# Feed-forward sums turned by VectorE in 32x32 blocks, stored in 128-byte pieces, with units of 960 tokens in a row

## The chip, the core and the metric

The kernel runs on one core of one Trainium2 chip. The metric is the time of one execution in microseconds (us), the median of three runs. The core has TensorE (PE in the profile, with PEld for its weight loads), VectorE (DVE), ScalarE (ACT), GpSimd (POOL) and SyncE (SP), which here issues all DMA transfers. SBUF is the working memory, PSUM the memory that TensorE writes.

## The reference

The input x has 4 batches of 12480 tokens with 128 features; there are 32 inducing vectors. All is in float32.

```python
def mab(q, kv):
    s = scale * (q @ kv.transpose(0, 2, 1))
    s = s - s.max(-1, keepdims=True)
    a = np.exp(s)
    a /= a.sum(-1, keepdims=True) + 1e-09
    return a @ kv
h = mab(I, x)                      # first attention: 32 inducing vectors over 12480 tokens
y = mab(x, h).reshape(49920, 128)  # second attention: each token over the 32 rows of h
hid = np.maximum(y @ w_in, 0.0)    # feed-forward, 128 -> 2048
out = (hid * hid) @ w_out          # 2048 -> 128
```

## The kernel before

The 49920 tokens are cut into 52 units of 960, 13 per batch. A unit is two blocks of 480 tokens. For each unit there are three stages.

First attention (class `First`): x is loaded as a tile xn of 120 partitions with 8 tokens each, turned by TensorE to xt (features on partitions; L463, copied by L270), scored against the inducing vectors (L478), exponentiated with a running maximum, turned back (L512) and multiplied with xn (L536). After the 13th unit of a batch `first_end` joins the parts to hT, and folds it into the feed-forward's first weights: hw = hT x w_in (L632 to L641). Second attention (class `Second`) scores a unit's tokens against hT (L674), evicts and turns the scores (ss, L693), does the softmax with 120 tokens on the partitions (L700 to L721, tile d, whose last product is L721), and turns it back (PE ap, L752). A high part of the result in reduced-precision float (fp32r) and the low remainder go to sw (L270 and L762). Sixteen small DMAs (L768) copy sw, over partitions, into st: four times the 32 weights of a token, high and low, stacked on 128 partitions. Feed-forward (`ffn_block`): for each block, 16 matmuls h (L896) of 480 columns read st and hw; ScalarE applies relu (L908) and the square (L924) to g; VectorE splits g into hi (L929) and lo (L934); 48 matmuls (L973) sum hi x wo_hi, hi x wo_lo and lo x wo_hi into one PSUM bank op, features on partitions.

What then happens to op is what the change touches. `done` copies op to SBUF (ot, by ScalarE or VectorE, L270), `turn` turns it on TensorE with four transposes (otp, L993), `turned` copies them to osb on VectorE (L270), and once both blocks of a unit are there, `store` writes the unit with one DMA (L1007). In the last unit the blocks are stored apart (L1011), and the very last block is handled in two halves (L1021 to L1039).

Tokens are numbered so that a partition of xn and osb holds 8 tokens that follow one another in memory:

```python
x_v = x.rearrange("b (p j) c -> b p j c", p=TS)             # L228, TS = 120
out_v = out.rearrange("(b p j) c -> b p j c", b=B, p=TS)    # L229
```

so a load and a store move 120 pieces of 4 KB per unit. The two blocks of a unit take alternate groups of 120 tokens, which is why an h matmul reads st in four runs (`s["st", u][:, :, k, :]`).

The order of the work on every engine is written out ahead by a planner (class `Plan`, `run` at L84). Each piece of work is added with its engine or a choice of engines ("ACT|DVE"), an assumed length in ns, what it needs, which buffers it takes, and a due time. The planner picks for each engine, among what can start, the piece with the earliest due time. Due times of unit w hang on `t_main + w * PERIOD`, with PERIOD 32000. The numbers are only for ordering: on the chip each engine runs its list in order and waits on semaphores. SP too runs its list in order, so a DMA that waits holds those behind it. The program gives its DMAs eight semaphores in turn, and a DMA waits until the one eight places ahead of it has landed.

Second attention of a unit is started only once the first h matmul of the unit before it has been issued (`begun`, in `narrow`); its st is needed by that next unit's first h matmul. st and the output tiles have two buffers each, as has op.

## Time and profile before

| | |
|---|---|
| median of 3 runs | 1729.77 us (1728.26 to 1730.32) |
| profiled execution, its span | 1730.0 us |
| granted TensorE clock, mean | 0.995 |
| PE busy | 1706.0 us, 99% of the span |
| DVE busy | 1651.4 us, 95% |
| ACT busy | 1605.6 us, 93% |
| DMA packets | 56935, 82.06 MB, 18.1% of 16 engines on SP's queue |

A row of the groups gives line, engine, operation, tiles as written <- read, shape, count, then the busy time in us, the mean ns of one, and the idle time ahead of them. The chain of waits is followed back from the last instruction; its rows give start, length and what held the time. A window row gives for a stretch the busy time of each engine (and the number of instructions), the granted clock, the DMA engines' share and GB/s. A timeline row gives start and length in us. SPq is the issue of a DMA by SP.

### The profile page before, as it was taken

The page shows a single profiled execution, that of the slowest core. Times are in us where ns is not written, and L with a number is a line of the kernel's source. Part 1 is how long each engine was busy: PE and PEld are TensorE (multiplying, and loading weights), DVE is VectorE, ACT ScalarE, POOL GpSimd, SP SyncE. Part 2 cuts the span into 40 slices and gives each one's busy share as a digit, 9 for nine tenths or more (in the row PEclk, how much of TensorE's full clock was granted, in tenths as well). Part 3 has the DMA queues.
Part 4 walks back from the last instruction along what each step waited for, and adds up shares of the span by engine and source line. Part 5 has one row for each costly group of instructions (what it writes and reads, how often), then busy time and mean ns, then how long its engine had stood idle before and what let it go on. Part 6 is the DMA issues. An engine that isn't in the chain of part 4 may idle for free.

```text
span 1730.0 us, 25326 instructions
## 1 busy us (share of the span) xinstructions
PE 1706.0 (99%) x9527; PEld 1416.2 (82%) x9527; DVE 1651.4 (95%) x1734; ACT 1605.6 (93%) x1686; POOL 58.3 (3%) x57
## 2 busy tenths in 40 slices
PE   7899999999999999999999999999999999999998
PEld 5588888888788888888878888888887888888887
DVE  5999999999999999999999999999999999999998
ACT  6699999999989999999988999999998999999997
POOL 0000000000000000000000000000000000000000
PEclk9899999999999999999999999999999999999999
DMA  9121111111121111111212111111110111111010
GB/s 234 51 55 47 51 43 44 52 45 43 36 57 47 50 43 46 52 45 43 53 29 58 49 43 47 51 44 44 42 28 24 35 35 40 30 37 33 24 46 23
DMA packets 56935, 82.06 MB, mean 47 GB/s; under 512 B 14790, under 2 KB 43942, under 8 KB 56814
## 3 DMA queue, kind: packets, MB, share of 16 engines
q1 hardware_dynamic: 56814, 80.46, 18.1%
q8 instruction: 75, 1.23, 0.3%
q14 instruction: 46, 0.38, 0.1%
HBM read 29.77 MB, written 25.56 MB: 32 GB/s over the span
## 4 chain that ended last, share of the span: by engine, by line
PE 94%; DVE 2%; ACT 1%; DMA 1%; SPq 1%; issue 0%; ACTq 0%; DVEq 0%
PE op L973 61%; PE h L896 21%; PE otp L993 3%; PE xtp L463 2%; PE na L674 2%; PE nb L536 1%; PE na L478 1%; PE ep L512 1%; PE s2t L693 1%; PE ap L752 1%; PE wp L632 1%; DVE lo L934 0%; SPq L768 0%; DVE hi L929 0%; PE sp L478 0%
## 5 line engine op out<-in xcount | busy, mean ns | idle before, releaser
L934 DVE TENSOR_TENSOR lo<-g,hi 128x1920 fp32r<-128x1920 f32 (+1 forms) x419 | 895.2, 2137 | 16.8 <-DVE hi L929 0.5
L908 ACT ACTIVATE g<-h 128x960 f32<-128x960 f32 x832 | 794.7, 983 | 62.5 <-PE h L896 60.8
L924 ACT ACTIVATE g<-g 128x1920 f32<-128x1920 f32 (+1 forms) x419 | 758.8, 1811 | 4.0
L896 PE MATMUL h<-st,hw 128*128 128x480 f32 x1664 | 523.5, 392 | 2.4 <-DMA st<-sw 1.2
L929 DVE CAST hi<-g 128x1920 fp32r<-128x1920 f32 (+1 forms) x419 | 480.0, 1146 | 20.0 <-PE op L973 9.6
L973 PE MATMUL op<-hi,wo_lo 128*128 128x480 f32 x1664 | 495.7, 383 | 0.0
L973 PE MATMUL op<-hi,wo_hi 128*128 128x480 f32 x1664 | 458.8, 386 | 0.0
L973 PE MATMUL op<-lo,wo_hi 128*128 128x480 f32 x1664 | 436.6, 382 | 0.0
L973 PEld LDWEIGHTS op<-lo,wo_hi 128*128 128x128 f32 x1664 | 311.4, 188 | 52.6 <-issue 1.0
L973 PEld LDWEIGHTS op<-hi,wo_lo 128*128 128x128 f32 x1664 | 308.9, 188 | 53.0 <-issue 4.6
L896 PEld LDWEIGHTS h<-st,hw 128*128 128x128 f32 x1664 | 303.0, 189 | 57.1 <-issue 11.7
L973 PEld LDWEIGHTS op<-hi,wo_hi 128*128 128x128 f32 x1664 | 304.1, 188 | 45.9 <-issue 0.9
L715 POOL TENSOR_SCALAR z<-z 120x8 f32<-120x8 f32 x51 | 57.6, 1130 | 1606.6 <-DVE z L711 1606.6
L270 DVE COPY osb<-otp 120x512 f32<-120x512 f32 x103 | 70.2, 682 | 0.1
L463 PE MATMUL xtp<-ident,xn 120*128 120x120 f32 x416 | 61.9, 276 | 4.3 <-DMA xn<-in_x_dram 3.6
L463 PEld LDWEIGHTS xtp<-ident,xn 120*128 120x128 f32 x416 | 51.2, 146 | 17.5 <-issue 3.7
L993 PE MATMUL otp<-ident,ot 128*120 128x128 f32 x412 | 61.8, 272 | 0.5 <-DVE ot L270 0.5
L993 PEld LDWEIGHTS otp<-ident,ot 128*120 128x120 f32 x412 | 50.4, 137 | 12.8 <-DVE ot L270 1.5
L270 ACT COPY xt<-xtp 128x480 f32<-128x480 f32 x71 | 40.3, 572 | 13.4 <-PE xtp L463 13.4
L270 ACT COPY ot<-op 128x480 f32<-128x480 f32 x65 | 37.1, 570 | 0.8 <-PE op L973 0.8
L536 PE MATMUL nb<-xn,et 120*32 120x128 f32 x752 | 34.1, 280 | 0.0
L674 PE MATMUL na<-xt,hT 128*32 128x240 f32 x416 | 32.7, 387 | 0.4 <-DVE hT L270 0.4
(117 smaller groups left out, 650.6 us busy)
## 6 DMA issues: line engine op xcount, KB each, us to landing
xn<-in_x_dram SPq DMA_DIRECT2D x52, 480.0 KB, 4.3
st<-sw SPq DMA_DIRECT2D x816, 30.0 KB, 1.9
out_dram<-osb SPq DMA_DIRECT2D x51, 480.0 KB, 3.4
hi_i<-in_moe_w_in_dram SPq DMA_DIRECT2D x2, 512.0 KB, 13.5
lo_i<-in_moe_w_in_dram SPq DMA_DIRECT2D x2, 512.0 KB, 15.6
hi_o<-in_moe_w_out_dram SPq DMA_DIRECT2D x2, 512.0 KB, 11.9
lo_o<-in_moe_w_out_dram SPq DMA_DIRECT2D x2, 512.0 KB, 9.8
out_dram<-osb SPq DMA_DIRECT2D x1, 240.0 KB, 2.6
```

Of the source, the lines that this page charges most:

```text
L270: ENG[task.by](dst, src)
L463: nc.tensor.transpose(v["tp"][:, t * TS:(t + 1) * TS], self.xn[:, 4 * k + t, :], ident[:TS, :TS])
L536: nc.tensor.matmul(where[q * M:(q + 1) * M, :], self.et[:, k, q * M:(q + 1) * M], self.xn[:, 2 * q + k, :], start=(k == 0), stop=(k == 1),)
L674: nc.tensor.matmul(where[q * M:(q + 1) * M, :], self.s["hT"][:, :M], self.s["xt"][self.u][:, q * 2 * TS:(q + 1) * 2 * TS], start=True, sto ...
L715: E.tensor_scalar(v["z"], v["z"], 1e-9, 0.0, ALU.add, ALU.add)
L896: nc.tensor.matmul(c["hp"][:, l, :BLK].rearrange("p (q t) -> p q t", q=Q), s["hw"][:, f * P:(f + 1) * P], s["st", u][:, :, k, :], start=Tr ...
L908: nc.scalar.activation(g, h, AF.Relu)
L924: nc.scalar.activation(v["g"][:, h], v["g"][:, h], AF.Square)
L929: ENG[by](v["hi"][:, h], v["g"][:, h])
L934: engine.tensor_sub(v["lo"][:, h], v["g"][:, h], v["hi"][:, h])
L973: nc.tensor.matmul(w["op"][:, :BLK], wo[:, 4 * j + l, :], v[name][:, l, :], start=(j == x == 0 and l == 0), stop=(j == NQ - 1 and x == 5 a ...
L993: nc.tensor.transpose(tp[:TS, q * P:(q + 1) * P], w["ot"][:, q * TS:(q + 1) * TS], ident)
```

## The change

Units become 960 tokens in a row, and blocks their halves of 480. x is loaded with token u*960 + j*120 + p on partition p, in pieces of 512 bytes (960 of them per unit, 120 x 8). An h matmul reads the half's 480 columns in one run. The feed-forward sums are no longer copied and turned by TensorE: VectorE's transpose reads op from PSUM and writes ob in SBUF, with each 32x32 block turned in itself. After it partition 32g + t, place (r, c), holds token 32r + t, feature 32g + c. So a token's row lies on four partitions, and a block is stored by four DMAs, one for each g, each with 32 partitions x 15 pieces of 32 floats (128 bytes). Each block is stored by itself. The very last block is turned and stored in two parts (8 and 7 rows of blocks). PERIOD goes from 32000 to 30500, and the planner is told 570 ns for the transpose and 2000 for a store. In the first unit, whose st is made without DMAs, both blocks now wait for both halves of st (`self.ready = [last] * 2`).

```diff
+S = 32
+NR = BLK // S
...
-    PERIOD, START, T_MAIN, NARROW, STEP = 32000.0, 2600.0, 44000.0, -9000.0, 3000.0
+    PERIOD, START, T_MAIN, NARROW, STEP = 30500.0, 2600.0, 44000.0, -9000.0, 3000.0
...
-    x_v = x.rearrange("b (p j) c -> b p j c", p=TS)
-    out_v = out.rearrange("(b p j) c -> b p j c", b=B, p=TS)
+    x_v = x.rearrange("b (u j p) c -> b u p j c", j=NT, p=TS)
+    out_v = out.rearrange("(b u k r t) (g c) -> b u k g t r c", b=B, k=2, t=S, r=NR, g=P // S)
...
-                nc.sync.dma_start(self.xn, x_v[b, :, u * NT:(u + 1) * NT, :])
+                nc.sync.dma_start(self.xn, x_v[b, u])
...
-                self.ready = t1
+                self.ready = [last] * 2
...
-                        c["hp"][:, l, :BLK].rearrange("p (q t) -> p q t", q=Q), s["hw"][:, f * P:(f + 1) * P], s["st", u][:, :, k, :],
+                        c["hp"][:, l, :BLK], s["hw"][:, f * P:(f + 1) * P],
+                        s["st", u][:, 2 * k:2 * k + 2].rearrange("p q k t -> p (q k t)"),
...
-        def done():
-            w["ot"] = att.tile([P, BLK], F32, tag="ot", name=f"ot_{n}")
-            copy(td, w["ot"], w["op"][:, :BLK])
-
-        def turn():
-            w["tp"] = tp = bank(f"otp_{n}")
-            for q in range(Q):
-                nc.tensor.transpose(
-                    tp[:TS, q * P:(q + 1) * P], w["ot"][:, q * TS:(q + 1) * TS], ident
-                )
-
-        def turned():
...
-        def store():
-            nc.sync.dma_start(out_v[b, :, u * NT:(u + 1) * NT, :], s["osb", u])
...
+        def turn(rows):
+            if "ob" not in w:
+                w["ob"] = att.tile([P, NR, S], F32, tag="ob", name=f"ob_{n}")
+            nc.vector.transpose(
+                w["ob"][:, rows].rearrange("p r c -> p (r c)"), w["op"][:, rows.start * S:rows.stop * S]
             )
 
+        def store(rows):
+            for g in range(P // S):
+                nc.sync.dma_start(out_v[b, u, k, g, :, rows], w["ob"][g * S:(g + 1) * S, rows])
 
         end = t0 + PERIOD / 2 + 8000
...
+        parts = [slice(0, 8), slice(8, NR)] if (b, u) == units[-1] and k == 1 else [slice(0, NR)]
+        t = None
+        for rows in parts:
+            t = add("DVE", 70 + 500 * (rows.stop - rows.start) / NR, lambda rows=rows: turn(rows), end + OT_DUE, [last, t],
+                    reads=[bo], late=LATE_OT if len(parts) == 1 else 0)
+            add("SP", 2000, lambda rows=rows: store(rows), end + 6000, [t])
```

The planner's lists change with it. The counts: PE loses the 416 otp transposes and nothing else; DVE loses 104 osb copies, 39 ot copies and 42 of 45 sw casts, and gains 103 transposes of 128x480, two shorter ones and two xt copies; ACT loses 66 ot copies, one osb copy and two xt copies and gains the 42 sw casts; SP has 420 stores where it had 54. Three places show the order. In names, the numbers after a tile are unit, block and group of four (h: pair) where it has them, and a last running number.

On PE, the end of unit 6 of a batch, around the first h matmul of unit 7 (h_7_0_0). Before:

```order
L973 MATMUL op_6_1_11379<-hi_6_1_0_11344,wo_hi 128x480 x2
L896 MATMUL h_6_1_6_11383<-st_6_10991,hw_8941 128x480 x2
L973 MATMUL op_6_1_11379<-hi_6_1_0_11344,wo_hi 128x480 x2
L973 MATMUL op_6_1_11379<-hi_6_1_0_11344,wo_lo 128x480 x2
L993 MATMUL otp_6_0_11395<-ident,ot_6_0_11386 120x128 x4
L896 MATMUL h_6_1_7_11400<-st_6_10991,hw_8941 128x480 x2
L973 MATMUL op_6_1_11379<-hi_6_1_0_11344,wo_lo 128x480 x2
L973 MATMUL op_6_1_11379<-lo_6_1_0_11358,wo_hi 128x480 x4
L973 MATMUL op_6_1_11379<-hi_6_1_1_11377,wo_hi 128x480 x2
L896 MATMUL h_7_0_0_11416<-st_7_11308,hw_8941 128x480 x2
L973 MATMUL op_6_1_11379<-hi_6_1_1_11377,wo_hi 128x480 x2
L674 MATMUL na_8_11425<-xt_8_7121,hT_8939 32x240 x4
```

and now:

```order
L976 MATMUL op_6_1_11191<-hi_6_1_0_11156,wo_hi 128x480 x4
L898 MATMUL h_6_1_7_11200<-st_6_10793,hw_8814 128x480 x2
L976 MATMUL op_6_1_11191<-hi_6_1_0_11156,wo_lo 128x480 x4
L976 MATMUL op_6_1_11191<-lo_6_1_0_11165,wo_hi 128x480 x2
L898 MATMUL h_7_0_0_11213<-st_7_11104,hw_8814 128x480
L676 MATMUL na_8_11215<-xt_8_7005,hT_8812 32x240 x4
```

h_7_0_0 stands after 10 op matmuls of block 6_1 instead of 14, and no otp set stands ahead of it. ap_7, from which second attention's result for unit 7 comes, stands behind the twelfth op matmul of block 6_0 and h_6_1_0 in both. So between ap_7 and h_7_0_0 there are 46 op matmuls instead of 50, 14 h matmuls and two xtp sets as before, and no otp set instead of one.

On DVE, between the last product of unit 7's softmax (d_7) and the low part of its sw. Before:

```order
L721 TENSOR_TENSOR d_7_11191<-d_7_11191,z_2_7_11220 120x256
L270 COPY osb_5_11101<-otp_5_1_11245 120x4x128
L929 CAST hi_6_0_2_11269<-g_6_0_2_11208 128x1920
L270 CAST sw_7_11284<-ap_7_11266 128x240
L934 TENSOR_TENSOR lo_6_0_2_11287<-g_6_0_2_11208,hi_6_0_2_11269 128x1920
L762 TENSOR_TENSOR sw_7_11284<-ap_7_11266,sw_7_11284 128x240
```

and now:

```order
L723 TENSOR_TENSOR d_7_10999<-d_7_10999,z_2_7_11014 120x256
L992 STREAM_TRANSPOSE ob_5_1_11066<-op_5_1_10880 128x480
L932 CAST hi_6_0_2_11071<-g_6_0_2_11025 128x1920
L272 COPY xt_8_11082<-xtp_8_0_11083 128x480
L764 TENSOR_TENSOR sw_7_11090<-ap_7_11073,sw_7_11090 128x240
L937 TENSOR_TENSOR lo_6_0_2_11100<-g_6_0_2_11025,hi_6_0_2_11071 128x1920
```

The low part of sw stands ahead of the long lo instead of behind it, the high part is ACT's, and an xt copy stands between.

On SP, some two units of the second batch. Before:

```order
L1007 DMA out_dram<-osb_4_6629 120x1024
L768 DMA st_6_6836<-sw_6_6812 32x240 x16
L422 DMA xn_9_6976<-in_x_dram 120x1024
L1007 DMA out_dram<-osb_5_6946 120x1024
L768 DMA st_7_7153<-sw_7_7129 32x240 x16
```

and now:

```order
L998 DMA out_dram<-ob_4_1_6678 32x15x32 x4
L770 DMA st_6_6716<-sw_6_6702 32x240 x16
L998 DMA out_dram<-ob_5_0_6823 32x15x32 x4
L424 DMA xn_9_6869<-in_x_dram 120x8x128
L998 DMA out_dram<-ob_5_1_6989 32x15x32 x4
L770 DMA st_7_7027<-sw_7_7013 32x240 x16
```

Four stores of a block stand right ahead of the sixteen st transfers. So it is for 37 units; in the last eleven, the st transfers come first.

More of the change, by code (lines that the diff above doesn't have):

```diff
@@ L225, in bank @@
         return ps_m.tile([P, 512], F32, tag="m", name=name)
-    x_v = x.rearrange("b (p j) c -> b p j c", p=TS)
-    out_v = out.rearrange("(b p j) c -> b p j c", b=B, p=TS)
+    x_v = x.rearrange("b (u j p) c -> b u p j c", j=NT, p=TS)
+    out_v = out.rearrange("(b u k r t) (g c) -> b u k g t r c", b=B, k=2, t=S, r=NR, g=P // S)
     def load_x(b, u, pool):
         xn = pool.tile([TS, NT, C], F32, tag="xn", name=f"xn_{b}_{u}")
-        nc.sync.dma_start(xn, x_v[b, :, u * NT:(u + 1) * NT, :])
+        nc.sync.dma_start(xn, x_v[b, u])
         return xn
@@ L1006, in store @@
-        def store():
-            nc.sync.dma_start(out_v[b, :, u * NT:(u + 1) * NT, :], s["osb", u])
-        def store_block():
-            pair = out_v[b, :, u * NT:(u + 1) * NT, :].rearrange("t (q k) c -> t k q c", k=2)
-            nc.sync.dma_start(pair[:, k], s["osb", u].rearrange("t (q k) c -> t k q c", k=2)[:, k])
-        end = t0 + PERIOD / 2 + 8000
-        if HALVES and (b, u) == units[-1] and k == 1:
-            for h in range(2):
-                def done_h(h=h):
-                    if h == 0:
-                        w["ot"] = att.tile([P, BLK], F32, tag="ot", name=f"ot_{n}")
-                    c = slice(h * 2 * TS, (h + 1) * 2 * TS)
-                    ENG["ACT" if h else "DVE"](w["ot"][:, c], w["op"][:, c])
-                def turn_h(h=h):
-                    w["tp", h] = tp = bank(f"otp_{n}_{h}")
-                    for q in range(2):
-                        nc.tensor.transpose(
-                            tp[:TS, q * P:(q + 1) * P], w["ot"][:, (2 * h + q) * TS:(2 * h + q + 1) * TS], ident
-                        )
-                def rows(x, h=h):
-                    return x.rearrange("t (q k) c -> t k q c", k=2)[:, k, 2 * h:2 * h + 2]
-                def turned_h(h=h, rows=rows):
-                    ENG["ACT" if h else "DVE"](
-                        rows(s["osb", u]), w["tp", h][:TS, :2 * P].rearrange("t (q c) -> t q c", q=2)
-                    )
-                def store_h(rows=rows):
-                    nc.sync.dma_start(rows(out_v[b, :, u * NT:(u + 1) * NT, :]), rows(s["osb", u]))
-                bt = Buffer("m")
-                e = "ACT" if h else "DVE"
-                t = add(e, 300, done_h, end + h, [last], reads=[bo], late=0)
-                t = add("PE", 219, turn_h, end + 600, [t], takes=[bt], mode="t")
-                t = add(e, 330, turned_h, end + 1500, [t], reads=[bt], late=0)
-                add("SP", 1500, store_h, end + 6000, [t])
-            return w["begun"]
@@ L1048, in ffn_block @@
-        bt = Buffer("m")
-        td = add(OT[k], (455, 570), done, end + OT_DUE, [last], reads=[bo], late=LATE_OT)
-        t = add("PE", 437, turn, end + OTP_DUE, [td], takes=[bt], mode="t")
-        t = tt = s["out", u, k] = add(OB, (480, 600), turned, end + OSB_DUE, [t], reads=[bt])
-        if (b, u) == units[-1]:
-            add("SP", 1500, store_block, end + 6000, [t])
-        elif k == 1:
-            add("SP", 2000, store, end + 6000, [t, s["out", u, 0]])
+        def turn(rows):
[3 more added lines that the diff above has]
+                w["ob"][:, rows].rearrange("p r c -> p (r c)"), w["op"][:, rows.start * S:rows.stop * S]
+            )
```

5 lines of the change are left out of this document (removed).

## The prediction

> **What bounds the kernel now.** I read the page's busy shares and its chain first, then the windows of some units in the middle and at the end, then the chain inside one unit.
>
> ```profile
> span 1730.0 us, 25326 instructions
> PE 1706.0 (99%) x9527; PEld 1416.2 (82%) x9527; DVE 1651.4 (95%) x1734; ACT 1605.6 (93%) x1686; POOL 58.3 (3%) x57
> PE 94%; DVE 2%; ACT 1%; DMA 1%; SPq 1%; issue 0%; ACTq 0%; DVEq 0%
> ```
>
> ```profile
> core 0: us, PE busy (x) PEld busy (x) DVE busy (x) ACT busy (x) POOL busy (x), PEclk, DMA share, GB/s
> 806.00:838.00 32.00, 32.00 (x182) 26.85 (x182) 31.06 (x33) 30.44 (x31) 1.17 (x1) 1.00 0.18 47
> 838.00:870.00 32.00, 32.00 (x186) 26.68 (x189) 31.42 (x34) 30.66 (x32) 1.18 (x1) 1.00 0.19 48
> 1584.00:1614.00 30.00, 30.00 (x149) 25.21 (x148) 29.23 (x27) 29.03 (x28) 0.24 (x1) 1.00 0.12 32
> ```
>
> A unit (960 tokens) takes 32 us in the middle and 30 us at the end. TensorE (PE) is without a gap in each, at full granted clock; VectorE (DVE) has 0.6 to 0.9 us of air and ScalarE (ACT) 1.0 to 1.6. PE sets the end, but with little behind it: what PE sheds is gained only if DVE, ACT and the loop below follow. That loop is the second thing to read: a unit's second attention starts behind its predecessor's first feed-forward matmul and ends with the st transfers, for which the next unit's first h matmul waits.
>
> ```profile
> 806.19 0.68 PE h L896 x2
> 820.26 0.44 PE otp L993 x4
> 820.70 0.44 PE h L896 x2
> 821.14 1.30 PE op L973 x6
> 822.88 0.21 PE ap L752 x2
> 838.43 0.44 PE h L896 x2
> 822.70 0.35 SPq L1007 DMA_DIRECT2D out_dram<-osb  x1
> 824.08 11.76 SPq L768 DMA_DIRECT2D st<-sw  x16
> L768 SPq DMA_DIRECT2D st<-sw x816: 507/588/1570, 81.3 to 1684.0; - x164
> DMA to landing us min/median/max: 1.7/1.9/5.0
> PE h L896 <- DMA st<-sw: 1.2, 1, 1.2
> ```
>
> The first row and the one at 838.43 are the first h matmuls of two neighbouring units, 32.2 us apart. ap starts 15.55 us before the second. The sixteenth st issue ends at 835.84, so it began 0.59 earlier, and lands 1.9 after that, at 837.15: 1.3 us before h. PE waited visibly for st only once (1.2 us), but 1.3 us is all there is.
>
> **What PE sheds.** The four otp transposes of a block hold 0.44 us of the chain. There are 103 such sets (the 104th is the tail, below): 103 x 0.44 = 45.3 us. The order shows no other PE work added or removed. h now reads its operand in one run instead of four. In the rows above an h matmul holds 0.22 us and an op matmul, which reads one run, 0.217: I take nothing, and keep 1664 x 0.003 = 5 us of possible gain.
>
> **What DVE and ACT do.** These are the groups that go or move, and a short copy for the slope:
>
> ```profile
> L270 DVE COPY osb<-otp 120x512 f32<-120x512 f32 x103 | 70.2, 682 | 0.1
> L270 DVE COPY ot<-op 128x480 f32<-128x480 f32 x38 | 24.7, 649 | 0.0
> L270 ACT COPY ot<-op 128x480 f32<-128x480 f32 x65 | 37.1, 570 | 0.8 <-PE op L973 0.8
> L270 DVE CAST sw<-ap 128x240 fp32r<-128x240 f32 x45 | 18.0, 400 | 0.6 <-PE ap L752 0.5
> L270 DVE COPY ss<-na 128x240 f32<-128x240 f32 x52 | 20.7, 398 | 0.0
> ```
>
> DVE loses 103 osb copies (70.2), 38 ot copies (24.7) and, by the new order, 42 of the 45 sw casts (16.8, they go to ACT); it gains 103 transposes and two xt copies (1.3). The trace holds no DVE transpose. The nearest row reads the same 128x480 from the same bank: 649 ns. Below, one element a lane at the slope of the two copies, (649 - 398) / 240 = 1.05 ns a column, is 502 ns without any fixed part; above, a second pass is 649 + 502 = 1151 ns. I take 650. DVE: -111.7 + 1.3 + 67 = -43 us, 0.8 a unit, so some 30.4 of a new unit of 31.1 (32 - 0.88). ACT loses 65 x 570 = 37.1 and gains 42 x 0.42 = 17.6, hence 0.4 a unit less, 30.1 of 31.1. Both stay under PE by as much as before.
>
> The Trainium skill, "VectorE: DVE Perf Modes", section on the three transpose paths, gives 311 ns for a 128x128 bf16 transpose; with 352 more columns at the slope above this makes, as an estimate, 680 ns, and DVE would shed 40 us instead of 43. No run here shows it yet.
>
> **The loop.** Two things move in it. On PE the first h of the next unit now stands 4 op matmuls and one otp set closer behind ap: 4 x 0.22 + 0.44 = 1.3 us, so 14.2 us after ap instead of 15.55. On DVE and SyncE (SP):
>
> ```profile
> 821.65 0.42 DVE L721 TENSOR_TENSOR d<-d,z 120x256 f32<-120x256 f32 x1
> 821.99 0.68 DVE L270 COPY osb<-otp 120x512 f32<-120x512 f32 x1
> 822.59 1.15 DVE L929 CAST hi<-g 128x1920 fp32r<-128x1920 f32 x1
> 823.66 0.40 DVE L270 CAST sw<-ap 128x240 fp32r<-128x240 f32 x1
> 826.04 0.40 DVE L762 TENSOR_TENSOR sw<-ap,sw 128x240 fp32r<-128x240 f32 x1
> 827.48 0.66 DVE L270 COPY xt<-xtp 128x480 f32<-128x480 f32 x1
> 828.05 2.15 DVE L934 TENSOR_TENSOR lo<-g,hi 128x1920 fp32r<-128x1920 f32 x1
> ```
>
> Count from N, the start of the first row (the softmax's last product). Now the low part of sw starts at N + 4.39, st ends its issues at N + 14.19 and lands at N + 15.5, h comes at N + 16.8. In the new order there stand between N and low sw only the product (0.34 to the next start), the transpose (0.6), one hi (1.07) and one xt copy (0.57): low sw starts at N + 2.6 and ends at N + 3.0. The store must be issued first: four DMAs from N + 1.1 on, each 0.35 (the out row) to 0.59 (the st row, which also has 32 partitions), so SP is free at N + 2.5 to 3.5. One st issue, then 15 more at (835.84 - 826.44) / 15 = 0.63: last landing at N + 13.7 to 14.7. h now wants it at N + 1.23 + 14.2 = N + 15.5. Slack 0.8 to 1.8 against 1.3 now: the loop just follows. I allow 2 us for units that miss it.
>
> **The small pieces.** A block's store is 1920 pieces of 128 bytes where half a unit was 60 of 4 KB. The smallest pieces that the trace writes to DRAM are 512 bytes, in the last unit (480 pieces in one transfer, 240 in two):
>
> ```profile
> DMA packets 495, 0.25 MB, mean 70 GB/s; under 512 B 15, under 2 KB 495, under 8 KB 495
> q1 hardware_dynamic: 495, 0.25, 29.0%
> out_dram<-osb SPq DMA_DIRECT2D x1, 240.0 KB, 2.6
> out_dram<-osb SPq DMA_DIRECT2D x2, 120.0 KB, 2.0
> ```
>
> In that 3.5 us window 29% of 16 engines is 16.2 us for 480 pieces and 15 tiny ones: 33 ns a piece. From 240 to 480 pieces the landing moves by 0.6 us: 2.5 ns a piece over all engines, on 1.4 us that doesn't scale. So 1920 pieces land 1.4 + 4.8 = 6.2 us after the first issue, if a 128-byte piece costs what a 512-byte one does. It could cost a quarter, or more than one. This matters because the program gives its DMAs eight semaphores in turn, so the eighth st issue waits for the fourth store's landing: N + 7.3, while its own turn comes at N + 6.9 to 7.9. At 33 ns it just fits; cheaper pieces leave room.
>
> The Trainium skill, "DMA: Bandwidth & Descriptors", Specifications, says against this change that a transfer under 512 B makes the DMA read, modify and write. The trace has no data piece under 512 B, so no run here shows it; what it would do is the second rival.
>
> x now arrives in 512-byte pieces too. PE's waits for x are the first row here, small, and all at the start, where the DMA engines are full. The second row is the window 26:36, nearly all pieces of 4 KB, the third 36.6:44, nearly all of 1 KB:
>
> ```profile
> PE xtp L463 <- DMA xn<-in_x_dram: 3.6, 2, 3.1
> q1 hardware_dynamic: 709, 2.40, 99.9%
> q1 hardware_dynamic: 1639, 1.72, 84.3%
> ```
>
> 2.40 MB in 159.8 us of engine time is 15.0 KB/us; 1.72 MB in 99.8 us is 17.2; the 512-byte stores above moved 15.4. Small pieces down to 512 lose nothing, so I take 0, with -3 to +5 us kept.
>
> **Ends.** The first unit's h now waits for both stacked halves, one more copy of about 0.5 us. In the tail, copy, turn, copy and store become two transposes and eight stores:
>
> ```profile
> 1724.39 0.42 DVE ot L1021
> 1725.93 0.42 DVE osb L1034
> 1726.11 0.83 SPq L1039 DMA_DIRECT2D out_dram<-osb  x2
> ```
>
> Now: 1724.4 to the end at 1730.0, 5.6 us. Then: a transpose (0.42), eight issues of 0.41 and a landing of 2.0, about 5.8. No change.
>
> **Sum.** The profiled execution's 1730.0 is the runs' median, 1729.77, to within 0.3. 1730.0 - 45.3 + 2 + 0.5 = 1687.
>
> **Rivals.**
> *The store holds up the st transfers (slower).* Place: SP, store ahead of st, in the 37 units of the new order where it stands so. If a 128-byte piece costs twice 2.5 ns, the fourth store lands 11.0 us after the first issue, N + 12.1; the eighth st goes then, eight more follow at 0.63, the last lands at N + 18.4, 2.9 us after h wanted it. 37 x 2.9 = 107: 1794. It decides from the point where it eats 43 us, 1.2 a unit: 4.1 ns a piece, some 60 ns on an engine. The 33 ns for four times the bytes speaks against it, the missing row for it. The skill's rule named above would lead here.
> *DVE becomes the bound.* With the transpose at 1151 ns DVE needs 1.0 us more a unit, 31.4 of 31.1 in the middle and 29.4 of 29.2 at the end; with half of its present 0.6 us of air kept, 0.5 to 0.6 us are lost in each of 51 units, some 29 us: 1716. For it: DVE's 97%. Against: a copy of that size takes 649.
> *The loop sets the pace without slow pieces.* Stores whose issue costs 1 us instead of 0.35 to 0.59 put SP back to N + 5.1 and the landing to N + 16.4: 0.9 x 37 = 33 us lost, 1720.
> *The layouts do nothing* since PE waits elsewhere: windows at 100% and a chain that is 94% PE speak against it; 1730.
>
> **How the numbers follow.** Forecast 1687: 0.64 (its own range 1679 to 1703, from the -3 to +5 of x, the -5 of h and up to 0.3 us a unit in the loop). DVE as bound 0.08, loop 0.07, nothing 0.03, slow pieces 0.18. A measurement here tells 0.2%, 3.5 us, from no change. Faster: 0.64 + 0.08 + 0.06 = 0.78; same 0.03; slower 0.19. Low end 1678; the high end must take in some of the slow pieces, so 1750.
>
> **What would show it.** Right: no otp rows; PE at 100% with units of 31.1 and 29.2; STREAM_TRANSPOSE near 650 ns; packets of 128 bytes at 10 to 35 ns; "PE h <- DMA st" still a few us in all. Wrong: that wait in tens of us and SP waiting for DMA before st (slow pieces); out_dram landing beyond 8 us; DVE over 98% with PE waiting for lo or hi (DVE bound); a first h matmul later than now (start).

## Result and the profile after

| | before | after |
|---|---|---|
| median of the runs | 1730.05 us (4 runs, 1728.26 to 1731.43) | 1698.13 us (4 runs, 1696.28 to 1700.61) |
| ratio, 95% interval | | 0.9816 (0.9805 to 0.9828) |
| span of the profiled execution | 1730.0 us | 1697.8 us |

The kernel became 32 us faster. The forecast was 1687 us; 11 us of the gain that it worked out did not come. The four runs of the changed kernel differ with the granted clock: two with a mean of 0.997 took 1696.3 and 1696.7 us, two with 0.993 and 0.992 took 1699.6 (the profiled one) and 1700.6. These are the lines of the page of the changed kernel that answer to those shown of before:

```profile
span 1697.8 us, 25129 instructions
PE 1663.3 (98%) x9111; PEld 1373.5 (81%) x9111; DVE 1612.1 (95%) x1656; ACT 1584.6 (93%) x1659; POOL 86.8 (5%) x57
...
DMA packets 299126, 82.08 MB, mean 48 GB/s; under 512 B 220380, under 2 KB 298492, under 8 KB 299004
...
HBM read 29.77 MB, written 25.56 MB: 33 GB/s over the span
PE 93%; DVE 2%; ACT 2%; DMA 1%; SPq 1%; issue 1%; DVEq 0%; ACTq 0%
```

PE still sets the end, with one per cent of the chain less than before. DVE shed 39 us (1651.4 to 1612.1), ACT 21. There are five times as many DMA packets, most of them under 512 bytes. The windows of a unit in the middle, of one at the end, and of a stretch with the start of the fourth batch (us of each engine and number of instructions, then clock, DMA share, GB/s):

```profile
800.00:831.00 31.00, 31.00 (x176) 26.12 (x175) 30.18 (x31) 30.11 (x31) 2.09 (x1) 1.00 0.24 49
1570.00:1600.00 30.00, 30.00 (x146) 25.13 (x145) 29.55 (x27) 29.45 (x27) 1.09 (x1) 1.00 0.17 34
1301.00:1328.00 27.00, 24.21 (x104) 18.10 (x103) 22.20 (x21) 20.84 (x21) 0.25 (x1) 0.94 0.22 44
```

PE has no gap in the first two. From first h matmul to first h matmul, middle units now take 31.07 to 31.12 us (before about 32.0 in most) and late ones 29.1 to 29.4 (before about 30.1). In the third row PE stands idle for 2.8 us, and the granted clock is 0.94: for 3.4 us it was at half, and only 8 matmuls fall in these, where some 15 would at the usual 0.22 us.

```profile
1312.70:1316.10 3.40, 3.33 (x8) 2.81 (x9) 3.31 (x4) 3.40 (x5) 0.00 (x0) 0.50 0.12 29
```

The trace of before has no such stretch there (1.00 from 1290 to 1390).

The difference between the two profiled executions falls into three stretches. The forecast's column comes from the terms of its sum.

| stretch | before | forecast | after | after against forecast |
|---|---|---|---|---|
| start to the first h matmul | 67.0 | 67.5 | 72.3 | +4.8 |
| first h to the end of the last op matmul | 1657.4 | 1614.1 | 1618.7 | +4.6 |
| last op matmul to the end | 5.6 | 5.8 | 6.8 | +1.0 |
| sum | 1730.0 | 1687 | 1697.8 | +10.4 |

(1657.4 - 45.3 + 2 = 1614.1.) The 4.6 us of the middle row are found at one place. The three units around the start of the fourth batch (the 38th to the 40th) took 32.38 + 37.75 + 26.80 = 96.9 us before and 32.36 + 41.22 + 26.53 = 100.1 after, where three times 0.88 less would be 94.3: 5.8 lost. The 2 us allowed for the loop were not needed, and 0.8 is left over. The starts of the second and third batch lost nothing: 38.99 + 31.98 + 31.11 = 102.1 before, 41.15 + 28.51 + 29.72 = 99.4 after, 2.7 less (the third is the same to 0.1).

In all runs a time is 1.7 or 1.8 us more than the span of the same execution, so the two medians differ by 31.9 and the two spans by 32.2.

The loop that the prediction counted through, in the timeline of the changed kernel (start us, length us; the last row is the first h matmul of the next unit):

```profile
807.13 0.68 DVE L992 STREAM_TRANSPOSE ob<-op 128x480 f32<-128x480 f32 x1
...
807.75 0.37 PE L754 MATMUL ap<-ident,d 120*128 120x120 f32 x2
807.84 1.93 SPq L998 DMA_DIRECT2D out_dram<-ob  x4
...
809.34 0.39 DVE L764 TENSOR_TENSOR sw<-ap,sw 128x240 fp32r<-128x240 f32 x1
...
809.87 10.02 SPq L770 DMA_DIRECT2D st<-sw  x16
...
821.89 0.38 PE L898 MATMUL h<-st,hw 128*128 128x480 f32 x1
```

The low part of sw ends 1.98 us after ap's start, just as SP has issued the four stores (809.77); the sixteen st issues end at 819.89, and h starts 14.14 us after ap: the prediction had 14.2. No wait of an h matmul for st is in the list of waits. The groups' row of the new operation, and the median landing of the stores:

```profile
L992 DVE STREAM_TRANSPOSE ob<-op 128x480 f32<-128x480 f32 (+1 forms) x105 | 70.1, 669 | 2.9 <-PE op L976 2.5
...
out_dram<-ob SPq DMA_DIRECT2D x412, 60.0 KB, 2.0
```

### The profile page after: what moved, and what is told of

Same layout as the page of the kernel before. It is cut to its first block, busy times and chain, and to the rows that moved or that the text cites. A ratio compares the mean times of both kernels' runs of the same rounds, so it can differ in the third digit from the quotient of the medians.

```text
span 1697.8 us, 25129 instructions
## 1 busy us (share of the span) xinstructions
PE 1663.3 (98%) x9111; PEld 1373.5 (81%) x9111; DVE 1612.1 (95%) x1656; ACT 1584.6 (93%) x1659; POOL 86.8 (5%) x57
## 3 DMA queue, kind: packets, MB, share of 16 engines
HBM read 29.77 MB, written 25.56 MB: 33 GB/s over the span
## 4 chain that ended last, share of the span: by engine, by line
PE 93%; DVE 2%; ACT 2%; DMA 1%; SPq 1%; issue 1%; DVEq 0%; ACTq 0%
PE op L976 63%; PE h L898 22%; PE xtp L465 2%; PE na L676 2%; PE nb L538 1%; PE na L480 1%; ACT g L911 1%; DMA lo_i<-in_moe_w_in_dram 1%; PE wp L634 1%; DMA xn<-in_x_dram 1%; PE s2t L695 1%; DVE lo L937 1%; PE ap L754 1%; SPq L424 1%; PE ep L514 1%
## 5 line engine op out<-in xcount | busy, mean ns | idle before, releaser
L911 ACT ACTIVATE g<-h 128x960 f32<-128x960 f32 x832 | 786.3, 980 | 49.4 <-PE h L898 46.5
L976 PE MATMUL op<-lo,wo_hi 128*128 128x480 f32 x1664 | 493.3, 385 | 0.5 <-DVE lo L937 0.5
L976 PE MATMUL op<-hi,wo_hi 128*128 128x480 f32 x1664 | 445.7, 386 | 0.8 <-DVE hi L932 0.8
L976 PE MATMUL op<-hi,wo_lo 128*128 128x480 f32 x1664 | 441.3, 381 | 0.0
L898 PEld LDWEIGHTS h<-st,hw 128*128 128x128 f32 x1664 | 310.1, 188 | 73.0 <-issue 13.9
L717 POOL TENSOR_SCALAR z<-z 120x8 f32<-120x8 f32 x51 | 86.1, 1688 | 1548.6 <-DVE z L713 1548.6
L992 DVE STREAM_TRANSPOSE ob<-op 128x480 f32<-128x480 f32 (+1 forms) x105 | 70.1, 669 | 2.9 <-PE op L976 2.5
L538 PEld LDWEIGHTS nb<-xn,et 120*32 120x32 f32 x752 | 25.2, 111 | 7.5 <-issue 0.8
L709 ACT ACTIVATE d<-d 120x256 f32<-120x256 f32 x52 | 21.6, 416 | 7.6 <-DVE d L706 7.6
L702 DVE TENSOR_REDUCE mx<-s2t 120x8 f32<-120x256 f32 x52 | 21.8, 419 | 5.1 <-PE s2t L695 4.7
```

Source lines behind the costliest of these rows:

```text
L538: nc.tensor.matmul(where[q * M:(q + 1) * M, :], self.et[:, k, q * M:(q + 1) * M], self.xn[:, 2 * q + k, :], start=(k == 0), stop=(k == 1),)
L717: E.tensor_scalar(v["z"], v["z"], 1e-9, 0.0, ALU.add, ALU.add)
L898: nc.tensor.matmul(c["hp"][:, l, :BLK], s["hw"][:, f * P:(f + 1) * P], s["st", u][:, 2 * k:2 * k + 2].rearrange("p q k t -> p (q k t)"), s ...
L911: nc.scalar.activation(g, h, AF.Relu)
L976: nc.tensor.matmul(w["op"][:, :BLK], wo[:, 4 * j + l, :], v[name][:, l, :], start=(j == x == 0 and l == 0), stop=(j == NQ - 1 and x == 5 a ...
L992: nc.vector.transpose(w["ob"][:, rows].rearrange("p r c -> p (r c)"), w["op"][:, rows.start * S:rows.stop * S])
```

## The experiments

A median stands beside that of the kernel before on the same chip in the same session. "After" is the changed kernel, and edits are made to it unless said otherwise.

| run | median us | before | ratio, 95% interval |
|---|---|---|---|
| after | 1698.13 | 1730.05 | 0.9816 (0.9805 to 0.9828) |
| e1 x in 2-KB pieces | 1712.44 | 1728.33 | 0.9905 (0.989 to 0.9919) |
| e2 PERIOD 32000 | 1706.37 | 1728.33 | 0.987 (0.9855 to 0.9884) |
| e3 st of the second block first | 1706.65 | 1728.33 | 0.9872 (0.9855 to 0.9888) |
| e4 each transpose twice | 1745.93 | 1728.33 | 1.0097 (1.0082 to 1.0112) |
| e5 before, x in 512-byte pieces | 1732.15 | 1729.83 | 1.0011 (1.0002 to 1.002) |
| e6 x in 1-KB pieces | 1695.73 | 1729.83 | 0.9803 (0.979 to 0.9817) |
| e7 stores in 64-byte pieces | 1704.34 | 1729.83 | 0.9849 (0.9833 to 0.9864) |
| e8 before, PERIOD 30500 | 1735.93 | 1729.83 | 1.0039 (1.0026 to 1.0051) |
| e9 1-KB pieces and another tail | 1693.88 | 1729.35 | 0.9794 (0.978 to 0.9807) |
| e10 e9 with PERIOD 31100 | 1697.32 | 1729.35 | 0.9812 (0.9798 to 0.9825) |
| e11 e9 with PERIOD 30000 | 1696.66 | 1729.35 | 0.9809 (0.9795 to 0.9822) |
| e12 transposes put back on PE | 1741.87 | 1729.9 | 1.0072 (1.0058 to 1.0086) |

### Is the gain PE's?

The last run (e12) puts the main term of the sum back, and nothing else.

```diff
             add("SP", 2000, lambda rows=rows: store(rows), end + 6000, [t])
+        if len(parts) == 1:
+            def again():
+                tp = bank(f"otp_{n}")
+                for q in range(Q):
+                    nc.tensor.transpose(
+                        tp[:TS, q * P:(q + 1) * P], w["ob"].rearrange("p r c -> p (r c)")[:, q * TS:(q + 1) * TS], ident
+                    )
+            add("PE", 437, again, end + OTP_DUE, [t], takes=[Buffer("m")], mode="t")
```

> The changed kernel with the work put back on TensorE that it shed: four transposes of 128x120 a block (of ob, into a PSUM bank that nobody reads) in the 103 blocks, behind the block's turn by VectorE. Nothing else is added; the result does not use them. Theory (PE sets the pace, so the 45 us are gained and lost on PE alone): middle units 31.1 + 0.88 = 32.0 us, late units 29.2 + 0.88 = 30.1, total 1698 + 45 = 1743, give or take 4. Rival (part of the gain comes from VectorE's 43 us of relief or from the shorter loop, and PE's work has room beside them): middle units below 31.7, total below 1730.

1741.87, 43.7 us above after, where 45 was expected. The row of the groups, and the windows of two middle and two late units:

```profile
L1011 PE MATMUL otp<-ident,ob 128*120 128x128 f32 x412 | 62.0, 273 | 1.2 <-DVE ob L992 1.2
```

```profile
717.57:782.31 64.74, 64.74 (x370) 54.74 (x368) 61.56 (x61) 62.31 (x65) 3.19 (x2) 1.00 0.24 48
1544.85:1604.97 60.12, 60.12 (x297) 50.48 (x296) 57.94 (x51) 57.55 (x53) 2.17 (x2) 1.00 0.17 34
```

PE is without a gap again. Units of the middle now alternate between 30.6 and 33.3 us (the pair shown is 32.72 + 32.02); the mean over nineteen of them in the second and third batch is 31.95, where after has 31.09 and before 31.91. Late units are at 29.99 (29.27 and 30.08). From the first unit to the last, the units start 41.3 us further apart, 0.81 a unit. So PE's work was the gain: the run gives it back to within 2 us with DVE, the layouts and the pieces as the change has them. DVE keeps its relief, and the kernel is still 12 us above before.

### Is VectorE next?

```diff
-            nc.vector.transpose(
-                w["ob"][:, rows].rearrange("p r c -> p (r c)"), w["op"][:, rows.start * S:rows.stop * S]
-            )
+            for _ in range(2):
+                nc.vector.transpose(
+                    w["ob"][:, rows].rearrange("p r c -> p (r c)"), w["op"][:, rows.start * S:rows.stop * S]
+                )
```

> The changed kernel with each VectorE transpose done twice to the same place (the second is of no use), so 103 x 0.6 us more work on VectorE that the planner knows nothing of: the load that a transpose of twice the length would have made. Theory: VectorE has 0.8 to 0.9 us of air in a unit of 31; 1.2 us more eats it and leaves 0.3 to 0.5 us a unit: 15 to 25 us, 1713 to 1723. Rival 1: VectorE already sets the pace beside TensorE: all 62 us appear, 1755 to 1760. Rival 2: VectorE's busy time contains waits and it has several us to spare: within 3 us of 1698.

1745.93, 47.8 us above after, between the two. The chain by engine, the doubled group, and two middle and two late units:

```profile
PE 50%; DVE 26%; issue 11%; ACT 7%; SPq 3%; DMA 2%; DVEq 0%; ACTq 0%
```

```profile
L993 DVE STREAM_TRANSPOSE ob<-op 128x480 f32<-128x480 f32 (+1 forms) x210 | 141.3, 673 | 6.5 <-PE op L976 2.9
```

```profile
711.90:775.33 63.43, 62.62 (x349) 52.15 (x348) 62.66 (x65) 59.61 (x63) 4.18 (x2) 1.00 0.23 47
1544.48:1605.81 61.33, 59.92 (x282) 47.80 (x280) 60.26 (x55) 57.32 (x53) 2.18 (x2) 1.00 0.17 33
```

Twice 0.67 us more a unit (1.34) lengthens a middle unit by 0.65 and a late one by 1.4. In the middle DVE could take on some 0.7 us a unit before PE starts to wait; at the end it could take on nothing, though it stood idle for 0.5 us in each late unit of after (57.58 us busy in 58.52). The rival with DVE as the bound was thus a mechanism that exists, and only its price was not met: two transposes of 1151 ns instead of 669 would be 0.96 us more a unit, of which, by this run, a middle unit would have paid some 0.3 and a late one all.

### Do the stores hold up the st transfers?

```diff
-                nc.sync.dma_start(out_v[b, u, k, g, :, rows], w["ob"][g * S:(g + 1) * S, rows])
+                for c in (slice(0, 16), slice(16, 32)):
+                    nc.sync.dma_start(out_v[b, u, k, g, :, rows, c], w["ob"][g * S:(g + 1) * S, rows, c])
```

> The changed kernel with each store cut into two of 64-byte pieces: eight DMAs and 3840 pieces a block. If a piece costs what it did at 128 bytes (12.7 ns), a block's pieces take 3.0 us over all engines and its eight issues 3 to 4 us; the st transfers behind them start 1.6 to 2 us later, and since the first eight st transfers have some 5 us to spare, little is lost: 1698 to 1705, units 31.1 to 31.2. Rival (the store holds up st, the prediction's rival, with its threshold now near): units of the 37 behind whose store st stands grow by 0.5 to 1.5 us, PE waits for st in h matmuls, 1717 to 1750.

1704.34, 6.2 us above after (the span is 6.8 longer), and none of it in the loop. Pieces are twice as many, a block's eight stores take 5.7 us from the first issue to the last landing (median; 3.4 us with four), and the st transfers of the 37 units start 2.1 us later in the median. Two middle units, beside those of after:

```profile
699.01:761.20 62.19, 62.19 (x349) 52.40 (x348) 60.54 (x61) 60.25 (x63) 4.18 (x2) 1.00 0.29 48
```

```profile
697.52:759.71 62.19, 62.19 (x350) 52.39 (x348) 60.53 (x61) 60.23 (x63) 4.18 (x2) 1.00 0.24 48
```

They are the same to 0.01 us. What was lost is 4.0 us in the tail (10.8 against 6.8: sixteen store issues one behind the other), 1.5 in a later start, and 1.3 at the start of the fourth batch. There the granted clock was at half for 6.8 us, where after had 3.4:

```profile
1313.50:1320.30 6.80, 6.04 (x15) 5.06 (x16) 6.67 (x5) 6.80 (x7) 0.00 (x0) 0.50 0.34 52
```

The start was not followed further; it scatters, with first h matmuls between 72.1 and 73.7 us in the five traces that have after's loads and PERIOD (after, e3, e4, e7, e12). The page's lines on packets and bytes:

```profile
DMA packets 505530, 82.14 MB, mean 48 GB/s; under 512 B 426780, under 2 KB 504892, under 8 KB 505404
HBM read 29.77 MB, written 25.56 MB: 32 GB/s over the span
```

The page gives the same 29.77 MB read with stores in pieces of 4 KB, 128 bytes and 64 bytes. That is just what the program's loads add up to (52 of 480 KB, 8 of 512 KB and one of 16 KB), so the line need not contain reads that a DMA engine might add by itself: whether small stores cause any, it does not tell. What they cost in time is in the packet records, below.

### Why the loop has room

The prediction let h wait for all sixteen st transfers. In the trace of after, each block's first h matmul waits on its own DMA semaphores: now that blocks are halves in a row, the first block of a unit needs only the first eight transfers, which land some 5 us before the sixteenth. In several of the 37 units the last of sixteen landed up to 1.2 us after the first h had begun, without a stall. With 64-byte pieces (e7) it did so in 26 of the 37, by up to 2.5 us, while the eighth still landed 2.1 us or more ahead of h, and no wait of h for st is in that list either. The next run sends the second block's eight first:

```diff
-                if q == 0:
+                if q == 2:
                     s["st", u] = ...
...
-            for q in range(Q):
+            for q in (2, 3, 0, 1):
```

> The changed kernel with the sixteen st transfers of a unit in another order: those for the second block first, those for the first block last. In the changed kernel a block reads only its own half of st, so the first h matmul waits for eight transfers, 5 us earlier than for all. Theory: this early half is what keeps the loop free (in 8 of 37 units the last of the sixteen landed 0.1 to 1.2 us after the first h had begun); with the needed half last those units wait, and the total rises by 5 to 20 us, to 1703 to 1718, with PE waits for st of that size. Rival: the loop had room for all sixteen, as the prediction reckoned (0.8 to 1.8 us): 1697 to 1700 and hardly a wait.

1706.65, 8.5 us above after. Of the 7.8 us between the two spans, 6 come in small steps over the units of the middle and 1.8 at the start of the fourth batch, where the granted clock was at half for 6.8 us as in e7. In the list of waits (us in all, times, longest) the first row stood at 5.2 in after; the second isn't there in after:

```profile
PE h L898 <- ACT g L911: 8.2, 13, 1.5
...
PE h L898 <- DMA st<-sw: 1.4, 2, 1.1
```

With 0.8 us more that the list puts down to issue, h waits 5.2 us more than in after. So the order of the sixteen matters and the early half keeps the loop free. The rest of the steps in the middle was not followed further.

### The start: pieces of x

The first h matmul comes 5.3 us later than before. These are SP's x loads in the first 40 us (shortest, median and longest issue in ns), the DMA packets of the 18 us from 12 on (packets, MB, share of 16 engines), and PE's wait. Before:

```profile
L422 SPq DMA_DIRECT2D xn<-in_x_dram x13: 324/325/724, 1.2 to 25.5; - x13
```

```profile
q1 hardware_dynamic: 1235, 4.43, 99.1%
```

After:

```profile
L424 SPq DMA_DIRECT2D xn<-in_x_dram x13: 358/1147/3930, 1.2 to 33.8; - x13
```

```profile
q1 hardware_dynamic: 5953, 3.78, 112.1%
```

```profile
PE xtp L465 <- DMA xn<-in_x_dram: 7.4, 6, 3.2
```

Issues are held for up to 3.9 us, the last x load of that stretch goes out at 33.8 instead of 25.5, and 3.78 MB are moved in the 18 us instead of 4.43 (211 GB/s instead of 247). Three runs test whether the pieces do it. The first took 2-KB pieces.

```diff
-    x_v = x.rearrange("b (u j p) c -> b u p j c", j=NT, p=TS)
+    x_v = x.rearrange("b (u k p j) c -> b u p k j c", k=2, p=TS, j=4)
...
-                    where[q * M:(q + 1) * M, :], indT,
-                    self.xt[:, q * 2 * TS:(q + 1) * 2 * TS], start=True, stop=True,
+                    where[q * M:(q + 1) * M, :].rearrange("m (j t) -> m j t", j=2), indT,
+                    self.xt[:, h * BLK:(h + 1) * BLK].rearrange("c (t j) -> c j t", j=4)[:, j:j + 2], start=True, stop=True,
```

> The changed kernel, but x comes in 104 x 120 pieces of 2 KB instead of 416 x 120 of 512 bytes: partition p of xn holds four tokens in a row of each half, TensorE writes its turned copy with a column step of 4, and the first attention's scores read with that step; all else as it was. Theory: the first h matmul came at 72.3 us instead of 67.0 because 512-byte pieces fill the DMA engines longer at the start (211 GB/s against 247 from 12 to 30 us) and hold SP's issues. Then the first h matmul goes back to 66 to 69 us, the issues of x fall back below 0.5 us, and the kernel takes 1692 to 1695 us. Rival: the later start is the order of the work, or the wait for both stacked halves: then the first h stays at 71 to 73 and the time at 1697 to 1699. If the column step slows the xtp or score matmuls, PE's xtp and na groups get longer and the time goes above 1698.

1712.44: slower than after, and not an answer. The first h came at 70.6 us, 1.7 earlier, but the scores that read xt in steps of four columns, ahead of the first h as in each unit, took 1.6 times as long:

```profile
L481 PE MATMUL na<-xt,indT 128*32 128x240 f32 x312 | 40.7, 598 | 0.0
```

(372 ns in after). Four of these a unit are 4 x 0.11 us on the path: middle units 31.5. The second run gives the kernel before the pieces alone, by four unused floats behind every 128 of the tile.

```diff
-                    [TS, NT, C], F32, tag="xn", name=f"xn_{self.n}"
-                )
+                    [TS, NT, C + 4], F32, tag="xn", name=f"xn_{self.n}"
+                )[:, :, :C]
```

> The kernel before with nothing changed but the x tile, which gets 4 unused floats behind every 128, so that x lands in pieces of 512 bytes (960 a unit) and not of 4 KB (120). The order of the work, the scores' reads and the tokens' places stay. Theory (the pieces are what the start lost): the issues of x in the first 25 us are held up to 2 to 4 us each, the first h matmul moves from 67.0 us to 71 to 72.5, and nearly all of it stays in the total: 1733 to 1737; middle units stay at 32.0. Rival (the start was lost by the other order of work or by the first unit's wait for both stacked halves): first h at 67 to 68, total 1729 to 1732.

```profile
q1 hardware_dynamic: 5878, 3.77, 112.3%
```

The first h comes at 72.1 us instead of 67.0, with the same rate as after in that window (211 GB/s): to within the scatter of the starts, the late start is the pieces, and neither the other order nor the wait for both stacked halves. But the total is only 2.3 us above before (expected: 3 to 7). In the kernel before the units that follow win some of it back: 4.2 us are left at the seventh unit, 2.5 at the thirteenth, 1.8 at the last. 1.4 of that comes in one unit (33.37 us before, 31.99 here), the one in which PE of the kernel before had its one wait for st. The third run takes pieces of 1 KB without a step in a moving operand.

```diff
-    x_v = x.rearrange("b (u j p) c -> b u p j c", j=NT, p=TS)
+    x_v = x.rearrange("b (u q p l) c -> b u p q l c", q=Q, l=2, p=TS)
...
-                        v["tp"][:, t * TS:(t + 1) * TS], self.xn[:, 4 * k + t, :], ident[:TS, :TS]
+                        v["tp"][:, :BLK].rearrange("c (q p l) -> c q l p", q=2, l=2)[:, t // 2, t % 2],
+                        self.xn[:, 4 * k + t, :], ident[:TS, :TS]
...
-                        v["ep"][:TS, k * P:(k + 1) * P], v["e"][:, k * TS:(k + 1) * TS], ident
+                        v["ep"][:TS, k * P:(k + 1) * P], v["e"].rearrange("p (t l) -> p l t", l=2)[:, k], ident
```

> The changed kernel with x in pieces of 1 KB: a partition holds two tokens that follow one another, four times; TensorE writes the turned x with a step of two columns, and the turn of the exponentials takes every second column as its weights. No matmul's moving operand gets a step. Theory (the number of pieces holds up the start): first h matmul at 69 to 71 us against 72.3, total 1694 to 1697 if the steps cost nothing; middle units 31.1. If a step in the weights or in the written columns costs like the one in the moving operand did, xtp or ep matmuls grow by 50% and a middle unit gains 0.2 to 0.4 us: total 1700 to 1715. Rival (pieces don't matter): first h at 72, total 1698.

```profile
q1 hardware_dynamic: 3308, 4.06, 106.3%
```

```profile
L465 PE MATMUL xtp<-ident,xn 120*128 120x120 f32 x416 | 61.0, 275 | 6.5 <-DMA xn<-in_x_dram 4.6
```

1695.73, first h at 69.6 us. The step in the written columns costs nothing (xtp 275 ns, 277 in after), middle units stay at 31.1. Of the 2.7 us won at the start all are still there at the end: its span is 3.2 us shorter than after's, its median 2.4. The intervals of the two ratios overlap, so the total alone would not show it; the first h matmul does: 69.2 to 70.0 us in the four traces with 1-KB pieces (e6, e9, e10, e11).

### The planner's period

The change also sets PERIOD from 32000 to 30500. Undone alone, and done alone on the kernel before:

```diff
-    PERIOD, START, T_MAIN, NARROW, STEP = 30500.0, 2600.0, 44000.0, -9000.0, 3000.0
+    PERIOD, START, T_MAIN, NARROW, STEP = 32000.0, 2600.0, 44000.0, -9000.0, 3000.0
```

> The changed kernel with the planner's PERIOD put back from 30500 to 32000, nothing else. Theory: the steady unit is PE's work alone (31.1 and 29.2 us), whatever PERIOD says, and PERIOD only moves what happens at the batch boundaries, where the third boundary lost some 5 us beside the other units; so units of 31.1 and 29.2 again and a total of 1690 to 1700. Rival: the tighter PERIOD is what lets h follow closer and gains part of the 32 us: then units of 31.5 or more and 1710 to 1720.

> The kernel before with the planner's PERIOD at 30500 instead of 32000, and nothing else. Theory (PERIOD only keeps the due times near the pace, and is worth little): middle units stay at 32.0, total within 4 us of 1729, with some of it at the batch boundaries. Rival (a good part of the gain, or of the 11 us lost at boundaries and ends, comes from PERIOD): the total moves by more than 5 us either way.

After with 32000: 1706.37, 8.2 us slower; before with 30500: 1735.93, 6.1 us slower. The expectations had 1690 to 1700 and within 4 us of 1729, so both undersized what PERIOD does; for e8 the rival came. Each kernel has the number that suits it of the two. With 32000 in both, the change is worth 22 us and not 32: middle units of after stay at 31.1 in e2 as well, and what moves are the starts of batches (table below).

### A version that is faster than both

In the tail of after the two transposes follow the last op matmul without delay, and then SP issues eight stores one behind the other:

```profile
1690.99 0.75 DVE L992 STREAM_TRANSPOSE ob<-op 128x256 f32<-128x256 f32 x2 [0.80 <-PE op L976]
1691.47 3.76 SPq L998 DMA_DIRECT2D out_dram<-ob  x8
```

This run keeps the 1-KB pieces of x, turns the last block in one piece, and splits its four stores over two queues:

```diff
-        parts = [slice(0, 8), slice(8, NR)] if (b, u) == units[-1] and k == 1 else [slice(0, NR)]
...
+        final = (b, u) == units[-1] and k == 1
+        t = add("DVE", 570, lambda: turn(slice(0, NR)), end + OT_DUE, [last], reads=[bo], late=0 if final else LATE_OT)
+        if final:
+            add("SP", 1000, lambda: store(nc.sync, (0, 1)), end + 6000, [t])
+            add("ACT", 1000, lambda: store(nc.scalar, (2, 3)), end + 6000, [t])
+        else:
+            add("SP", 2000, lambda: store(nc.sync, range(4)), end + 6000, [t])
```

> The changed kernel with x in pieces of 1 KB as in the run before it, and the very last block turned in one piece and stored by four DMAs, two issued by SP and two by ACT, instead of two turns and eight issues on SP. Theory (the tail's 6.8 us are eight issues of 0.4 to 0.5 one behind the other, and a landing): a turn of 0.7, two issues of some 0.5 on each queue and a landing of 2.4 make a tail of 4.0 to 4.6 us; total 1692 to 1694. Rival (the landing of the 128-byte pieces sets the tail, not the issues): tail 6 us or more, total 1695 to 1696.

```profile
1687.69 0.68 DVE L993 STREAM_TRANSPOSE ob<-op 128x480 f32<-128x480 f32 x1 [0.80 <-PE op L977]
1688.41 0.84 SPq L999 DMA_DIRECT2D out_dram<-ob  x2
1688.41 0.93 ACTq L999 DMA_DIRECT2D out_dram<-ob  x2
```

1693.88, the fastest of all, 4 us below after (the two intervals just touch; the spans are 1693.1 and 1697.8). The tail is 5.5 us instead of 6.8, between the two expectations: the issues end 2.6 us sooner behind the last op matmul than after's, but the landings became longer (2.2 to 2.8 us from the start of each issue, against 1.5 to 1.7), with all four side by side. Both the issues and the pieces' landing hold the tail.

Two more values of PERIOD, for the batch starts:

> The same with PERIOD 31100, the pace that the middle units have, instead of 30500. The 11 us that were lost against the prediction lie in part at the batch boundaries (some 2 us at each of the first two, 5.6 around the third), where the planner's list decides what stands ahead of what. Theory (the due times run ahead of the pace and crowd the boundaries): 1688 to 1692, with the first unit of a batch shorter than 41.2 us. Rival (as with 32000, where the boundaries got longer): 1694 to 1702.

> The same with PERIOD 30000. If longer periods lengthen the boundaries, as 32000 did, a shorter one may shorten them: 1689 to 1693. If 30500 is near the best, 1693 to 1705. Middle units stay at 31.1 in all of these, since PE has no gap there.

1697.32 and 1696.66: neither is better, though 31100 mends what it was meant to mend. Three units around the starts of the second and the fourth batch, in us (31100 and 30500 in the kernel with 1-KB pieces and the other tail):

| | second batch | fourth batch |
|---|---|---|
| before (32000) | 38.99 + 31.98 + 31.11 = 102.1 | 32.38 + 37.75 + 26.80 = 96.9 |
| after (30500) | 41.15 + 28.51 + 29.72 = 99.4 | 32.36 + 41.22 + 26.53 = 100.1 |
| e2 (32000) | 44.01 + 27.32 + 31.03 = 102.4 | 30.97 + 42.17 + 25.20 = 98.3 |
| e9 (30500) | 41.12 + 28.52 + 29.74 = 99.4 | 32.37 + 41.22 + 26.54 = 100.1 |
| e10 (31100) | 43.89 + 28.55 + 31.11 = 103.6 | 31.50 + 36.72 + 25.63 = 93.9 |

With 31100 the fourth batch starts in 93.9 us, what the forecast implied (94.3), but against 30500 the second loses 4.2 us, the third 3.0 and the last unit 1.4. So most of the 5.8 us at the fourth batch is a matter of the list's order there and not of any engine's work. What it looks like in after: the first h of the new batch stands behind all op matmuls of the old one, and ScalarE, which follows h, stands idle meanwhile. Its longest wait in that stretch:

```profile
1307.16 1.83 ACT L911 ACTIVATE g<-h 128x960 f32<-128x960 f32 x2 [8.51 <-PE h L898]
```

After that PE waits for ScalarE and VectorE to fill up again. PE's records tell how many op matmuls of the old batch were still to come when the first h of the new one went:

| | second batch | third batch | fourth batch |
|---|---|---|---|
| before | 24 | 24 | 16 |
| after, e9 | 12 | 12 | 0 |
| e2 | 0 | 0 | 0 |
| e10 | 0 | 0 | 18 |

In after, e2, e9 and e10, a second or third batch with none left starts in 102.4 to 103.6 us, with 12 left in 99.4; a fourth with none left in 98.3 to 100.1, with 18 left in 93.9. The granted clock has a part in it. e2, with none left at the fourth batch and no stretch of half clock there, took 1.8 us less than after; in e10 the second batch had 3.4 us of half clock and the third had none, at 103.6 and 102.4 us. So of the 5.8 us some 1.2 to 1.8 went with the clock, and 4 or more with the order. Which due time in the planner puts the order so, the runs do not tell; nor what brings the half clock, since PE stands idle for 2.8 us in those three units of after and of e2 alike.

## Why the prediction was right, and where it was off

**PE sheds 45.3 us: right.** Units of 31.1 and 29.2 were named, 31.07 to 31.12 and 29.1 to 29.4 came, and putting the work back (e12) cost 43.7. That h reads one run instead of four was worth nothing, as taken: 388 ns a matmul against 392, and the units leave no room for a gain.

**The transpose at 650 ns: right, 669.** The estimate worked out from the Trainium skill's figure ("VectorE: DVE Perf Modes", the three transpose paths), 680, agrees with the trace as well. DVE shed 39 us, not 43, and has 0.8 us of 31.0 free in the middle (forecast 0.7), ACT 0.9 (forecast 1.0). By e4 the air in the middle is real; late units had none, and a dearer transpose would have cost its whole excess there.

**The loop: harmless as forecast, for another reason, so this part was luck.** ap to h was right to 0.1 us. But "last landing" against h was the wrong comparison: h of the first block needs the first eight transfers only. Had it needed all sixteen, units would have missed it, as e3 shows. The allowance of 2 us was not used, and both rivals that went through SP had some 5 us more to eat than the prediction gave them. That is why doubling the pieces and issues (e7) still cost the loop nothing.

**Small pieces on the store: sized too dear.** 33 ns for a piece was taken from 512-byte pieces. The packet records of after give 12.7 ns on the average for 199680 pieces of 128 bytes, and in e7 9.6 ns for 64 bytes; a block lands 3.4 us after its first issue, not 6.2. Rival 1 needed 60 ns on an engine. The rule of the Trainium skill that stood against the change is that below 512 bytes the DMA reads, modifies and writes ("DMA: Bandwidth & Descriptors", Specifications). Whether it did so, no run here shows; 12.7 ns is what a piece took, whatever went on in it. By bytes the small pieces are slower all the same: 128 bytes in 12.7 ns are 10 KB/us, a 4-KB load in 229 ns has 18.

**x in 512-byte pieces: this term failed.** "Small pieces down to 512 lose nothing, so I take 0, with -3 to +5 us kept." It cost 5 us at the start, the end of the kept range, and e5 shows that the pieces are enough for it. A first h matmul later than before was one of the prediction's own signs of being wrong. The three rates that the step rested on came from 4-KB pieces in a full stretch, from 1-KB pieces in a stretch that was 84% full, and from a burst of stores. In the full stretch from 12 to 30 us the bytes per engine time are 4.43 MB / (18 x 16 x 0.991) = 15.5 KB/us for 4 KB, 4.06 / (288 x 1.063) = 13.3 where most pieces are 1 KB, and 3.78 / (288 x 1.121) = 11.7 where they are 512. Shares above 100% mean that packets overlap on an engine, so these are rates per packet time; the stretch itself moved 247, 227 and 211 GB/s. Loads of x became slower piece by piece, and since their issues were held up, the later ones started late as well.

**The ends.** The wait for both stacked halves was put at +0.5; e5, which lacks it, starts at 72.1 us and after at 72.3, and with the starts scattering by more than that, it can't be told from nothing. The tail was put at 5.8 and took 6.8: the eight issues took 3.76 us, 0.47 each, instead of 0.41, and from the end of the last issue to the end of the span it was 2.5 us, where a landing of 2.0 had been put. The last landing is at 1696.4, so 1.3 us of the tail lie behind it, as 1.4 did before; the prediction's sum had no term for that.

**Not in the prediction at all:** the 5.8 us at the start of the fourth batch. The sum took each unit's 0.88 us and assumed the rest of the list as it was; a planner that is given other lengths and another period orders the batch starts anew. With the old period (e2) the same change would have ended at 1706, above the forecast's own range.

The time lay in the upper part of the forecast's own range (1679 to 1703): about half of the distance for the reason that the range was given, x, and half for the batch start, for which nothing had been put. That it stayed inside owes something to luck: the 2 us kept for a loop that did not need them covered a part of the batch start.

## To carry to other kernels

When one engine is without a gap over whole units, work taken off it comes back almost whole (putting it back cost 43.7 us of 45.3 here), and can be counted from the chain's rows; the errors are then in the places that the steady unit doesn't show: the start, the batch boundaries and the tail. Price those from a stretch that is as full as the one they will stand in, since a rate measured where the DMA engines have air says little about a stretch where they have none. And when a layout changes, ask again which transfers a matmul really waits for.

## What was unexpected of the hardware

- Stores in pieces of 128 and 64 bytes: 12.7 and 9.6 ns a piece on an engine, against 40 ns for a 512-byte load and 229 ns for a 4-KB one in the same program. The packets of 4 bytes in the same trace take 9.1 ns, so 64 bytes cost hardly more than 4: the number of pieces, not of bytes, sets the time there. Yet 1920 pieces a block disappear beside the matmuls.
- With 960 pieces in a load, SP's issue of it is itself held, for up to 3.9 us, while the DMA engines are full; with 120 pieces it took 0.32 to 0.72.
- A matmul whose moving operand (fp32, 240 columns) is read in steps of four columns took 598 ns instead of 372. A step of two columns in what is written cost nothing (275 against 277). One in the weights lengthened their load from 138 to 192 ns, which lies beside other matmuls: the matmul itself took 288 ns against 282.
- The granted clock fell to 0.50 for 3.4 us (after, e10) or 6.8 (e3, e7) at a batch start in whose three units PE stood idle for 2.8 to 3.1 us. It did not in e2 with 2.8 us of idle time there, nor in e4 with 4.3.
